# A decode kernel with grouped attention and a dense branch: TensorE's program rolled into a loop over half-groups

## The chip, the cores and the metric

The kernel runs on one NeuronCore of a Trainium2 chip. A core has five engines, each with its own instruction stream: TensorE (PE in the profile; its weight loads are listed apart as PEld), VectorE (DVE), ScalarE (ACT), GpSimd (POOL) and SyncE (SP), which here issues most transfers. Sixteen DMA engines move data between HBM and the on-chip memory SBUF; TensorE writes to a second memory, PSUM. The metric is the device time of one execution in microseconds (us). A profiled execution gives one time beside its span, which runs from its first to its last instruction.

## The reference

One token is decoded. Its normalized row feeds two branches, and both are added to the row.

```python
xn = _layernorm(x)                                  # x: 1 x 512
q = (xn @ wq).reshape(1, 32, 128)                   # 32 heads of 128, wq 512 x 4096
# 8 groups of 4 heads share a key and a value cache of 65536 x 128 each (bf16)
p = softmax(einsum(q, k_cache[g]) * 128 ** -0.5)    # over 65536 keys, per head
A = concat_heads(p @ v_cache[g]) @ wo               # wo 4096 x 512
B = gelu(xn @ w1 + b1) @ w2 + b2                    # w1 512 x 1792, w2 1792 x 512
out = x + A + B
```

The two caches are 2 x 8 x 65536 x 128 values of 2 bytes, 268.4 MB, read once. The weights add 12 MB (wq 4.19, wo 4.19, w1 and w2 3.67).

## The kernel before

**How the order is made.** Python code records every instruction with the tiles that it reads and writes (`sch.op`, `sch.dma`); a recorder (`_Sched`) works out which semaphore waits are needed, and at the end each engine's list is written out in full, one instruction after another. So the order on each engine is that of the Python calls, and TensorE's program holds each of its matmuls once.

**Work and tiles.** For each of the 8 groups the 65536 keys come in 32 transfers of 2 MB (64 tiles of 128 keys x 128 values; line 339 issues them on SP), 16 for K and 16 for V. They land in `cbuf`, a ring of `NB = 8` slots: transfer n goes to slot n mod 8, once TensorE has finished with transfer n - 8. A slot holds two items of 32 tiles.

- A K item is transposed tile by tile on TensorE (line 430, into one of four PSUM tiles `pst`, eight tiles in each). DVE (line 441) or ACT (line 443) copies each filled `pst` to `ktbuf` (the profile's `R_kt`), in the ratio 5 to 3.
- Scores (line 456) multiply each transposed tile with the group's four query columns, two items behind the transposes. They collect in `pss`; DVE copies them to `scf` (line 469) and takes the maximum (line 473).
- When a group's scores are complete, TensorE and DVE turn the maxima into one negated maximum per head for all partitions (`gen_stats_1`, `gen_stats_2`: lines 494, 500, 506, 516, 522), and ACT computes the exps of four heads (line 533, 512 columns each) into `P_bf`, with their sums beside them.
- V items are multiplied with `P_bf` (line 547) and add up in `pB`. V runs one group behind K, so that items of K of group g and of V of group g - 1 alternate, two by two.
- After a group's last V item, TensorE sums the sums over the partitions (line 581), DVE normalizes (lines 585, 589), and 16 matmuls with the group's 512 KB of wo (line 601) add to `finT` (line 611).

The last phase has V items alone. The dense branch runs there: ACT issues the transfers of w1 and w2 (lines 367 and 370) into the transposed keys' memory once that is free; the pieces of the two products (lines 621 to 679) stand between the V items, and gelu between them on DVE and ACT. At the very end the group's epilogue, a transpose (line 782), a copy and the output's transfer (line 790) follow.

At the start SP issues three small rows (x, b1, b2; lines 306 to 310) ahead of the first K chunk, then wq in two transfers (line 351) and further K chunks. The layer norm runs on one partition, and the q projection (line 562) is done after the second K item.

The loop that writes all this down, cut to what sets the order:

```python
for n, it in enumerate(items):        # K,K,(V,V),K,K,(V,V),...
    if kind == "K":
        gen_transposes(i, b, u)
        gen_scores(i - LA); after_scores(i - LA)      # LA = 2
        if had_pending and softmax_q: softmax_q.pop(0)()
    else:
        if softmax_q and softmax_group[0] == g: flush_softmax()
        gen_pv(g, c, b, u)
        if ph == last_phase and pos_in_phase >= 1: ffn_pieces.pop(0)()
    dma_items_upto(dma_cap((n + 1) // NSUB + NB))     # ring of NB = 8
```

Of the kernel before, what the change touches and what calls it, by code (L numbers as in the profile page):

```python
# [5 lines left out]
BF = mybir.dt.bfloat16  # L6
# [4 lines left out]

_DEBUG = {}
# [137 lines left out]

def bass_parallel_sum__gqa_block_cached__dense_activation_gelu__decode_kernel(
# [22 lines left out]
    CH = 4096  # L174
    TPC = CH // 128
    NCH = S // CH
    NKCH = G * NCH
    TPG = NCH * TPC
    BPG = NCH // 4
    assert D % 128 == 0 and F % 128 == 0 and S % CH == 0 and NCH % 4 == 0  # L180
    assert A_k_cache.shape[3] == DH and H % G == 0 and KT == 4 and HPG == 4

    NSUB = 2
    TPD = NSUB * TPC
    NB = 8
    NKT = 4
    NPT = 4
    NPS = 2
    LA = 2
    VLAG = 1  # L190
    NPB = VLAG + 1
# [7 lines left out]
    _DEBUG["sched"] = sch  # L199
# [16 lines left out]
    xrow_bf = nc.alloc_sbuf_tensor("xrow_bf", [1, D], BF)  # L216
    xrow_f = nc.alloc_sbuf_tensor("xrow_f", [1, D], F32)
    junk_row = nc.alloc_sbuf_tensor("junk_row", [1, D], F32)
    st = nc.alloc_sbuf_tensor("st", [1, 8], F32)
    st2 = nc.alloc_sbuf_tensor("st2", [1, 8], F32)  # L220
    xn_row_bf = nc.alloc_sbuf_tensor("xn_row_bf", [1, D], BF)
    xnT_bf = nc.alloc_sbuf_tensor("xnT_bf", [128, KT], BF)
    b1row_bf = nc.alloc_sbuf_tensor("b1row_bf", [1, F], BF)
    b2row_bf = nc.alloc_sbuf_tensor("b2row_bf", [1, D], BF)
    qT_bf = nc.alloc_sbuf_tensor("qT_bf", [128, H], BF)
    h_f = nc.alloc_sbuf_tensor("h_f", [128, FC], F32)
# [6 lines left out]
    call = nc.alloc_sbuf_tensor("cbuf", [128, NB * TPD * DH], BF)  # L233
    cbuf = [call[:, i * TPD * DH:(i + 1) * TPD * DH].rearrange("p (t d) -> p t d", d=DH)
            for i in range(NB)]
    assert KT % NSUB == 0 and TPC * DH == H * DH
    NWQ = KT // NSUB
    WQ_SLOT0 = NB - NWQ
    wq_kt = [call[:, (WQ_SLOT0 * NSUB + kt) * TPC * DH:(WQ_SLOT0 * NSUB + kt + 1) * TPC * DH]
             for kt in range(KT)]  # L240
    wq_slot = [WQ_SLOT0 + kt // NSUB for kt in range(KT)]
    assert CH * NKT >= KT * F + FC * D
    R_kt = nc.alloc_sbuf_tensor("R_kt", [128, NKT * CH], BF)
    ktbuf = [R_kt[:, i * CH:(i + 1) * CH] for i in range(NKT)]
    w1_sb = R_kt[:, 0:KT * F].rearrange("p (kt f) -> p kt f", kt=KT)
    w2_sb = R_kt[:, KT * F:KT * F + FC * D].rearrange("p (fc n) -> p fc n", fc=FC)
    KT_RES_ALL = [f"ktbuf{kb}_{q}" for kb in range(NKT) for q in range(4)]
    wo_g = [nc.alloc_sbuf_tensor(f"wo_g{i}", [128, HPG, D], BF) for i in range(2)]
    scf = [nc.alloc_sbuf_tensor(f"scf{i}", [128, TPG * HPG], F32) for i in range(2)]
    scf_v = [scf[i][:, :].rearrange("p (t j) -> p t j", j=HPG) for i in range(2)]  # L250
    P_bf = [nc.alloc_sbuf_tensor(f"P_bf{i}", [128, TPG * HPG], BF) for i in range(NPB)]
    P_v = [P_bf[i][:, :].rearrange("p (t j) -> p t j", j=HPG) for i in range(NPB)]

    pmax = [nc.alloc_sbuf_tensor(f"pmax{i}", [128, HPG], F32) for i in range(2)]
    pmax_parts = [nc.alloc_sbuf_tensor(f"pmax_parts{i}", [128, BPG * HPG], F32) for i in range(2)]
    gmax4 = [nc.alloc_sbuf_tensor(f"gmax4_{i}", [HPG, 1], F32) for i in range(2)]
    diag4 = [nc.alloc_sbuf_tensor(f"diag4_{i}", [HPG, HPG], F32) for i in range(2)]
    negm = [nc.alloc_sbuf_tensor(f"negm{i}", [128, HPG], F32) for i in range(2)]
    sums = nc.alloc_sbuf_tensor("sums", [128, H], F32)
    rtot = nc.alloc_sbuf_tensor("rtot", [128, H], F32)  # L260
    oT_bf = nc.alloc_sbuf_tensor("oT_bf", [128, H], BF)

# [3 lines left out]
    pB = nc.alloc_psum_tensor("pB", [128, 512], F32)  # L266
    PA_Q = 0
    PA_H = 32
    PA_XN = 48
    PA_SB = 56  # L270
    PA_SUM = 64
# [4 lines left out]
    PB_O = 0  # L276

    csem = [sch.dsem(f"csem{i}") for i in range(NB)]
    sem_misc = sch.dsem("dmisc")
    sem_wq = sch.dsem("dwq")  # L280
    sem_w12 = sch.dsem("dw12")
    sem_out = sch.dsem("dout")


    sch.op(POOL, lambda: pool.memset(ident_bf[:, :], 0.0), writes=["ident_bf"])
    sch.op(
        POOL,
        lambda: pool.affine_select(
            out=ident_bf[:, :], in_=ident_bf[:, :], compare_op=ALU.not_equal, fill=1.0,
            base=0, pattern=[[-1, 128]], channel_multiplier=1,  # L290
        ),
        reads=["ident_bf"], writes=["ident_bf"],
    )
    sch.op(POOL, lambda: pool.memset(ident_f[:, :], 0.0), writes=["ident_f"])
    sch.op(
        POOL,
        lambda: pool.affine_select(
            out=ident_f[:, :], in_=ident_f[:, :], compare_op=ALU.not_equal, fill=1.0,
            base=0, pattern=[[-1, 128]], channel_multiplier=1,
        ),  # L300
        reads=["ident_f"], writes=["ident_f"],
    )
    sch.op(POOL, lambda: pool.memset(ones_f[:, :], 1.0), writes=["ones_f"])
    sch.op(POOL, lambda: pool.memset(finT[:, :], 0.0), writes=["finT"])

    sch.dma(SP, lambda: sp.dma_start(out=xrow_bf[:, :], in_=A_x[0]), sem_misc,
            writes=["xrow_bf"], total=48)
    sch.dma(SP, lambda: sp.dma_start(out=b1row_bf[:, :], in_=B_b1.rearrange("(o n) -> o n", o=1)),
            sem_misc, writes=["b1row"], total=48)
    sch.dma(SP, lambda: sp.dma_start(out=b2row_bf[:, :], in_=B_b2.rearrange("(o n) -> o n", o=1)),  # L310
            sem_misc, writes=["b2row"], total=48)

    NPH = G + VLAG
    items = []
    phase_start = []
    for ph in range(NPH):
        phase_start.append(len(items))
        for c in range(0, NCH + NSUB, NSUB):
            if ph < G and c < NCH:
                items.extend(("K", ph, c + s) for s in range(NSUB))  # L320
            if ph >= VLAG and c >= NSUB:
                items.extend(("V", ph - VLAG, c - NSUB + s) for s in range(NSUB))
    NITEMS = len(items)
    assert NITEMS == 2 * NKCH

    def item_src(it):
        kind, g, c = it
        cache = A_k_cache if kind == "K" else A_v_cache
        return cache[0, g, c * CH:(c + NSUB) * CH, :].rearrange("(p t) d -> p t d", p=128)

    next_item = [0]
    dma_hooks = {}

    def dma_items_upto(n_excl):
        while next_item[0] < min(n_excl, NITEMS // NSUB):
            n = next_item[0]
            b = n % NB
            src = item_src(items[n * NSUB])
            sch.dma(SP, lambda b=b, src=src: sp.dma_start(out=cbuf[b][:, :, :], in_=src),
                    csem[b], writes=[f"cbuf{b}"])  # L340
            for h in dma_hooks.get(n, ()):
                h()
# [511 lines left out]
```

## Time and profile before

| | |
|---|---|
| runs | 690.56 us median of 3 (689.59 to 691.35) |
| profiled execution | 689.94 us; span 688.1 us |
| TensorE's granted clock, mean | 0.792 |
| PE busy | 542.2 us, 12,732 matmuls and as many weight loads |
| DVE, ACT busy | 280.9 us, 243.9 us |
| read from HBM | 280.50 MB |

Rows that begin with a time range are windows: the range, its length, then for PE, PEld, DVE, ACT and POOL the busy us and the number of instructions, then the granted clock, the busy share of the DMA engines and GB/s. Rows "A <- B: x, n, m" are waits: A waited for B x us in all, n times, at most m; "issue" is waiting for nothing that the profile shows. Rows that begin with one time and one duration are the timeline. Rows with "|" are groups of instructions: busy us and mean ns of one, then the idle time ahead. In the rows on the queues, q1 is SP's, q10 ACT's, and q8 and q14 bring instructions: packets, MB, and the share of the sixteen engines' span that the packets took.

### The profile page before, as it was taken

The numbers are of one execution on the slowest core, as the hardware profiler recorded it, in microseconds if no ns is written. First come the engines' busy times: TensorE is split into PE (matmuls) and PEld (weight loads), VectorE is DVE, ScalarE is ACT, GpSimd is POOL, SyncE is SP. The second block draws the span as 40 slices with busy tenths as digits, with TensorE's granted clock in tenths as the row PEclk, the third lists the DMA queues.
The fourth block names the chain that finished last, engine by engine and source line by source line (L and its number), as shares of the span: only waits on it lengthen the run. The fifth ranks groups of instructions, "written<-read, shape, count | busy, mean of one in ns | idle before, by whom it ended". The sixth has DMA issues, their size and how long they took to land.

```text
span 688.1 us, 26439 instructions
## 1 busy us (share of the span) xinstructions
PE 542.2 (79%) x12732; PEld 531.3 (77%) x12732; DVE 280.9 (41%) x457; ACT 243.9 (35%) x266; POOL 1.3 (0%) x10
## 2 busy tenths in 40 slices
PE   3799588886978868887898868888688876887276
PEld 3788588886978868887798868888688876887265
DVE  2276444424444434435444244443344453444001
ACT  4255623325332353325333253332533234332200
POOL 0000000000000000000000000000000000000000
PEclk9799967757898889889879668897797777897555
DMA  8999999999999999999999999999999999999972
GB/s 345 426 426 422 424 423 418 422 427 424 423 416 424 425 422 418 423 424 424 424 417 426 422 424 420 418 426 424 427 418 422 421 425 425 421 424 421 425 310 110
DMA packets 23352, 282.19 MB, mean 410 GB/s; under 512 B 2251, under 2 KB 6349, under 8 KB 6350
## 3 DMA queue, kind: packets, MB, share of 16 engines
q1 hardware_dynamic: 22958, 276.84, 95.7%
q10 hardware_dynamic: 288, 3.67, 1.3%
q8 instruction: 99, 1.62, 1.0%
q14 instruction: 7, 0.06, 0.0%
HBM read 280.50 MB, written 0.00 MB: 408 GB/s over the span
## 4 chain that ended last, share of the span: by engine, by line
PE 64%; DMA 21%; issue 7%; ACT 6%; DVE 1%; SPq 0%
PE pst L430 37%; DMA cbuf<-in_A_k_cache_dram 18%; PE pss L456 12%; PE pB L547 12%; ACT P_bf L533 5%; DMA R_kt<-in_B_w_dram 3%; PE pA L621 1%; PE pA L601 0%; PE pA L494 0%; PE pA L516 0%; PE pA L630 0%; ACT R_kt L443 0%; DVE R_kt L441 0%; PE pA L581 0%; PE pA L661 0%
## 5 line engine op out<-in xcount | busy, mean ns | idle before, releaser
L430 PE MATMUL pst<-ident_bf,cbuf 128*128 128x128 bf16 x4096 | 319.7, 249 | 39.0 <-issue 28.2
L443 ACT ACTIVATE R_kt<-pst 128x1024 bf16<-128x1024 bf16 x192 | 196.6, 1024 | 387.4 <-PE pst L430 387.4
L430 PEld LDWEIGHTS pst<-ident_bf,cbuf 128*128 128x128 bf16 x4096 | 294.2, 114 | 44.6 <-issue 40.1
L441 DVE COPY R_kt<-pst 128x1024 bf16<-128x1024 bf16 x320 | 212.5, 687 | 246.6 <-PE pst L430 246.3
L547 PE MATMUL pB<-P_bf,cbuf 128*128 128x4 bf16 x4096 | 117.5, 165 | 60.3 <-ACT P_bf L533 38.7
L547 PEld LDWEIGHTS pB<-P_bf,cbuf 128*128 128x128 bf16 x4096 | 111.5, 99 | 62.4 <-ACT P_bf L533 39.3
L456 PE MATMUL pss<-qT_bf,R_kt 128*128 128x4 bf16 x4096 | 125.4, 165 | 12.6 <-issue 12.4
L456 PEld LDWEIGHTS pss<-qT_bf,R_kt 128*128 128x128 bf16 x4096 | 121.5, 98 | 13.7 <-issue 13.5
L533 ACT ACTIVATE P_bf<-scf,negm 128x512 bf16<-128x512 f32 x32 | 40.8, 1424 | 6.9 <-DVE negm L522 6.9
L473 DVE TENSOR_REDUCE pmax_parts<-scf 128x4 f32<-128x512 f32 x32 | 34.3, 1071 | 1.1
L469 DVE COPY scf<-pss 128x512 f32<-128x512 f32 x32 | 22.1, 691 | 16.7 <-PE pss L456 16.7
L585 DVE RECIPROCAL rtot<-pA 128x4 f32<-128x4 f32 x8 | 1.5, 182 | 43.4 <-PE pA L581 43.4
L611 DVE TENSOR_TENSOR finT<-pA,finT 128x4 f32<-128x4 f32 x8 | 1.3, 162 | 43.5 <-PE pA L601 43.5
L621 PE MATMUL pA<-xnT_bf,R_kt 128*128 128x1 bf16 x56 | 5.4, 201 | 15.9 <-DMA R_kt<-in_B_w_dram 15.9
L621 PEld LDWEIGHTS pA<-xnT_bf,R_kt 128*128 128x128 bf16 x56 | 4.4, 153 | 16.0 <-issue 15.9
L639 DVE COPY h_f<-pA 128x14 f32<-128x14 f32 x1 | 0.2, 172 | 28.4 <-PE pA L630 28.4
L648 ACT ACTIVATE g_t<-g_t 128x14 f32<-128x14 f32 x1 | 0.2, 215 | 31.2 <-DVE g_t L646 31.2
L533 ACT ACTIVATION_READ_ACCUMULATOR P_bf<-scf,negm 128x1 f32 x32 | 8.1, 253 | 0.0
L562 PE MATMUL pA<-xnT_bf,cbuf 128*128 128x1 bf16 x128 | 3.5, 165 | 4.3 <-DMA cbuf<-in_A_wq_dram 4.3
L562 PEld LDWEIGHTS pA<-xnT_bf,cbuf 128*128 128x128 bf16 x128 | 3.4, 102 | 4.5 <-DMA cbuf<-in_A_wq_dram 4.5
L410 PE MATMUL pA<-ident_bf,xn_row_bf 1*128 1x1 bf16 x4 | 0.3, 172 | 7.4 <-ACT xn_row_bf L403 7.4
L410 PEld LDWEIGHTS pA<-ident_bf,xn_row_bf 1*128 1x128 bf16 x4 | 0.2, 113 | 7.4 <-ACT xn_row_bf L403 7.4
(58 smaller groups left out, 57.6 us busy)
## 6 DMA issues: line engine op xcount, KB each, us to landing
cbuf<-in_A_k_cache_dram SPq DMA_DIRECT2D x64, 2048.0 KB, 29.6
cbuf<-in_A_v_cache_dram SPq DMA_DIRECT2D x64, 2048.0 KB, 30.4
cbuf<-in_A_wq_dram SPq DMA_DIRECT2D x2, 2048.0 KB, 14.5
wo_g<-in_A_wo_dram SPq DMA_DIRECT2D x8, 512.0 KB, 27.8
R_kt<-in_B_w_dram ACTq DMA_DIRECT2D x2, 1792.0 KB, 18.6
xrow_bf<-in_A_x_dram SPq DMA_DIRECT2D x1, 1.0 KB
b1row_bf<-in_B_b_dram SPq DMA_DIRECT2D x1, 3.5 KB
b2row_bf<-in_B_b_dram SPq DMA_DIRECT2D x1, 1.0 KB
```

Source lines behind the costliest of these rows:

```text
L430: lambda tb=tb, slot=slot, b=b, t=t, u=u: pe.transpose(pst[tb][:, slot * 128:(slot + 1) * 128], cbuf[b][:, u + t, :], ident_bf[:, :]),
L441: fn = (lambda tb=tb, dst=dst: dve.tensor_copy(out=dst, in_=pst[tb][:, :]))
L443: fn = (lambda tb=tb, dst=dst: act.activation(out=dst, in_=pst[tb][:, :], func=ACTF.Copy))
L456: lambda sb=sb, slot=slot, kb=kb, t=t, g=g: pe.matmul(pss[sb][:, slot * HPG:(slot + 1) * HPG], lhsT=ktbuf[kb][:, t * 128:(t + 1) * 128], r ...
L469: sch.op(DVE, lambda sb=sb, dst=dst: dve.tensor_copy(out=dst, in_=pss[sb][:, :]), reads=[f"pss{sb}"], writes=[f"scf{gp}_{k4}"])
L473: lambda gp=gp, k4=k4, dst=dst: dve.tensor_reduce(out=pmax_parts[gp][:, k4 * HPG:(k4 + 1) * HPG], in_=dst.rearrange("p (t j) -> p j t", j= ...
L533: lambda gp=gp, gq=gq, g=g, j=j: act.activation(out=P_v[gq][:, :, j], in_=scf_v[gp][:, :, j], func=ACTF.Exp, bias=negm[gp][:, j:j + 1], sc ...
L547: lambda g=g, c=c, b=b, t=t, gp=gp, u=u: pe.matmul(pB[:, PB_O + g * HPG:PB_O + (g + 1) * HPG], lhsT=cbuf[b][:, u + t, :], rhs=P_v[gp][:, c ...
L562: lambda h=h, kt=kt: pe.matmul(pA[:, PA_Q + h:PA_Q + h + 1], lhsT=wq_kt[kt][:, h * DH:(h + 1) * DH], rhs=xnT_bf[:, kt:kt + 1], start=(kt = ...
L585: sch.op(DVE, lambda hs=hs: dve.reciprocal(out=rtot[:, hs], in_=pA[:, PA_SUM:PA_SUM + HPG]), reads=["pA"], writes=[f"rtot{g}"])
L611: lambda: dve.tensor_tensor(out=finT[:, :], in0=pA[:, PA_AT:PA_AT + KT], in1=finT[:, :], op=ALU.add),
L621: lambda fc=fc, kt=kt: pe.matmul(pA[:, PA_H + fc:PA_H + fc + 1], lhsT=w1_sb[:, kt, fc:F:FC], rhs=xnT_bf[:, kt:kt + 1], start=(kt == 0), st ...
```

## The change

The kernel is rewritten around units. A unit is half a group: 32768 keys, four K chunks and four V chunks of 2 MB, so there are 16 units.

- TensorE's program for units 1 to 15 (K of unit u, V of unit u - 1) is recorded 15 times as before, then folded into one body, and written out once inside a loop of 15 rounds (`_fold`, `_emit_loop`). Semaphore values that grow from round to round stand in registers, which are added to between the waits. Unit 0 and the end stand outside. The other engines' programs are written out in full as before.
- Addresses in the body must not change, so slots are fixed: K chunk c of a unit in slot c, V chunk c in slot 4 + c. The transposed keys keep a ring of four, the queries of a unit are copied to one tile `q_cur`, and V adds up in one tile `pO`, which is copied out per unit (`keep_o`).
- Each unit has its own maximum, exps (256 columns) and sums. The two halves of each group are merged at the end: factors exp(min - negm) per half, the sum of the weighted sums, and weighted outputs, on DVE with one exp on ACT.
- wq, w1 and w2 lie at first in the V slots; SP issues them behind the first and the second K chunk, and the dense branch runs within unit 0. wo is kept whole in SBUF, loaded in four pieces of 1 MB by the end of unit 10. All 128 output products of the earlier units stand in the last stage, ahead of the last V chunk.
- The layer norm works on columns: x and b1 come in as columns, x and b2 also as rows, through four small transfers on ACT's queue.

The diff, cut to the parts that set the order:

```diff
+def _emit_loop(eng_obj, ops, growth, n):
...
+    with eng_obj.Fori(0, n):
+        for waits, fn, pub in ops:
+            for s, v in waits:
+                r, now = at[s]
+                if v != now:
+                    eng_obj.reg_add(r, r, v - now)
+                    at[s][1] = v
+                eng_obj.wait_ge(s, r)
+            ins = fn()
+            if pub is not None:
+                ins.then_inc(pub[0], pub[1])
+        for r, step in steps:
+            eng_obj.reg_add(r, r, step)
...
+    def unit(u, first):
...
+        k_block(0)
+        if not first:
+            stats_1()
+        k_block(1)
+        done_chunk("K", 0)
+        if not first:
+            stats_2(u - 1)
+        else:
+            qproj()
+            issue_chunks()
+        load_q(u)
+        k_block(2)
+        scores(u, 0)
+        k_block(3)
+        scores(u, 1)
+        done_chunk("K", 1)
+        v_block(0)
+        v_block(1)
+        if first:
+            ffn1()
+        else:
+            done_chunk("V", 0)
...
+    marks = []
+    unit(0, True)
+    for u in range(1, NU):
+        marks.append(len(PE.ops))
+        unit(u, False)
+    marks.append(len(PE.ops))
...
+    pv(2, 0)
+    wo_part(oT_bf, "oT", list(range(H)))
+    pv(2, 1)
+    pv(3, 0)
+    pv(3, 1)
...
         @block.tensor
         def _(e):
-            replay(PE, e)
+            folded, growth = _fold([PE.ops[a:b] for a, b in zip(marks, marks[1:])])
+            _emit(e, PE.ops[:marks[0]])
+            _emit_loop(e, folded, growth, len(marks) - 1)
+            _emit(e, PE.ops[marks[-1]:])
```

In the rows below a line number is that of the kernel in question, "x32" counts equal instructions in a row, and a wait names its semaphore: `csem` and `dwq` count transfers, `prog_dve`, `prog_act` and `prog_pe` count an engine's instructions.

TensorE before, where a group's softmax falls due (L494 and L516 are its statistics, L547 the V products, which wait for ACT's exps):

```order
L456 MATMUL pss<-qT_bf,R_kt 128x4 x32
L494 MATMUL pA<-ident_f,pmax 4x128 [waits prog_dve]
L430 MATMUL pst<-ident_bf,cbuf 128x128 [waits prog_dve]
L430 MATMUL pst<-ident_bf,cbuf 128x128 x7
L430 MATMUL pst<-ident_bf,cbuf 128x128 [waits prog_act]
```

```order
L456 MATMUL pss<-qT_bf,R_kt 128x4 x32
L516 MATMUL pA<-diag_1,ones_f 128x4 [waits prog_dve]
L547 MATMUL pB<-P_bf,cbuf 128x4 [waits csem2,prog_act]
L547 MATMUL pB<-P_bf,cbuf 128x4 x31
L601 MATMUL pA<-oT_bf,wo_g 128x1 [waits dwo0]
```

TensorE after, the loop's first rows (L210 enters the loop, L215 adds to a register, L538 and L548 are the statistics of the unit before):

```order
L210 UNCONDITIONAL_BRANCH
L484 MATMUL pst<-ident_bf,kv 128x128 [waits csem0]
L484 MATMUL pst<-ident_bf,kv 128x128 x31
L538 MATMUL pA<-ident_f,pmax 4x128 [waits prog_dve]
L215 REGISTER_ALU
L484 MATMUL pst<-ident_bf,kv 128x128 [waits prog_dve]
```

```order
L548 MATMUL pA<-diag,ones_f 128x4 [waits prog_dve]
L215 REGISTER_ALU
L484 MATMUL pst<-ident_bf,kv 128x128 [waits csem1,prog_act]
L484 MATMUL pst<-ident_bf,kv 128x128 x7
L215 REGISTER_ALU
```

The statistics now stand once, in the loop; between the second of them and the first V products lie two blocks of transposes and two of scores (before, nothing); registers are added to between the groups of eight transposes.

TensorE at the end of the program, before:

```order
L547 MATMUL pB<-P_bf,cbuf 128x4 x32
L547 MATMUL pB<-P_bf,cbuf 128x4 [waits csem6]
L547 MATMUL pB<-P_bf,cbuf 128x4 x63
L547 MATMUL pB<-P_bf,cbuf 128x4 [waits csem7]
L547 MATMUL pB<-P_bf,cbuf 128x4 x63
L581 MATMUL pA<-sums,ones_f 128x4 [waits prog_dve]
L601 MATMUL pA<-oT_bf,wo_g 128x1 [waits dwo1,prog_dve]
```

and after (L573 are the V products, L770 those with wo, L788 the final transpose):

```order
L573 MATMUL pO<-P_bf,kv 128x4 [waits csem6]
L573 MATMUL pO<-P_bf,kv 128x4 x31
L770 MATMUL pA<-oT_bf,wo_sb 128x1 [waits dwo,prog_dve]
L770 MATMUL pA<-oT_bf,wo_sb 128x1 x127
L573 MATMUL pO<-P_bf,kv 128x4 x32
L573 MATMUL pO<-P_bf,kv 128x4 [waits csem7]
L573 MATMUL pO<-P_bf,kv 128x4 x63
L770 MATMUL pA<-oL_bf,wo_sb 128x1 [waits prog_dve]
L770 MATMUL pA<-oL_bf,wo_sb 128x1 x15
L788 MATMUL pA<-ident_f,finT 4x128 [waits prog_dve]
```

The sums' product has moved ahead of these rows, 128 products with wo now stand between the two halves of the third V chunk, and 16 remain at the end.

SP at the start of the program, before:

```order
L306 DMA xrow_bf<-in_A_x_dram 1x512
L308 DMA b1row_bf<-in_B_b_dram 1x1792
L310 DMA b2row_bf<-in_B_b_dram 1x512
L339 DMA cbuf<-in_A_k_cache_dram 128x8192
L351 DMA cbuf<-in_A_wq_dram 128x8192 x2
L339 DMA cbuf<-in_A_k_cache_dram 128x8192 x5
```

and after:

```order
L407 DMA kv<-in_A_k_cache_dram 128x8192
L414 DMA kv<-in_A_wq_dram 128x16384
L407 DMA kv<-in_A_k_cache_dram 128x8192
L418 DMA kv<-in_B_w_dram 128x7168
L420 DMA kv<-in_B_w_dram 128x7168
L407 DMA kv<-in_A_k_cache_dram 128x8192 x2
L407 DMA kv<-in_A_k_cache_dram 128x8192 [waits prog_pe] x2
L407 DMA kv<-in_A_v_cache_dram 128x8192
```

The first K chunk is now the first transfer on SP, and the dense weights come behind the second one.

More of the change, by code (lines that the diff above doesn't have):

```diff
@@ L323, in bass_parallel_sum__gqa_block_cached__dense_activation_gelu__decode_kernel @@
[L323 to L342, printed above, removed]
-            next_item[0] += 1
@@ new lines, in stats_2 @@
+    def stats_2(u):
+        k, us = u % 2, slice(u * HPG, (u + 1) * HPG)
+        sch.op(PE, lambda: pe.matmul(pA[:, PA_SB:PA_SB + HPG], lhsT=ones_f[0:HPG, 0:128],
+                                     rhs=diag4[0:HPG, 0:HPG], start=True, stop=True),
+               reads=["diag", "ones_f"], writes=["pA"])
+        sch.op(DVE, lambda us=us: dve.tensor_scalar(out=negm[:, us], in0=pA[:, PA_SB:PA_SB + HPG],
+                                                    scalar1=-1.0, scalar2=None, op0=ALU.mult),
+               reads=["pA"], writes=[f"negm{u}"])
+        for j in range(HPG):
@@ L545, in gen_pv, with pv @@
+                reads=[f"negm{u}"] + [f"scf{k}_{b}" for b in range(NPS)],
+                writes=[f"P_{j}", f"sums{u}_{j}"],
+            )
+    def pv(c, s):
+        b = slot_of["V"] + c
+        for t in range(TPB):
+            tt = s * TPB + t
+            gt = c * TPD + tt
             sch.op(
                 PE,
[L547 to L552 removed]
@@ L618, in gen_ffn1_piece, with ffn1 @@
+        slot_free[NC] = slot_free[NC + 1] = True
+    def ffn1():
+        for fc in range(FC):
             for kt in range(KT):
```

868 lines of the change are left out of this document (402 added, 466 removed).

## The prediction

> **What bounds the kernel now.** I read the page's first sections, then the busy times by window at both ends of the run, then PE's waits.
>
> ```profile
> span 688.1 us, 26439 instructions
> PE 542.2 (79%) x12732; PEld 531.3 (77%) x12732; DVE 280.9 (41%) x457; ACT 243.9 (35%) x266; POOL 1.3 (0%) x10
> DMA  8999999999999999999999999999999999999972
> GB/s 345 426 426 422 424 423 418 422 427 424 423 416 424 425 422 418 423 424 424 424 417 426 422 424 420 418 426 424 427 418 422 421 425 425 421 424 421 425 310 110
> q1 hardware_dynamic: 22958, 276.84, 95.7%
> q8 instruction: 99, 1.62, 1.0%
> HBM read 280.50 MB, written 0.00 MB: 408 GB/s over the span
> ```
>
> The DMA engines are full from the second slice to the 38th and move about 423 GB/s; 280.5 MB at that rate are 663 us. So the transfers bound the kernel, and the other 25 us lie at the ends: about 3 at the start (345 GB/s in slice 1) and the rest in the last two slices (310 and 110 GB/s). The windows of the end show what is missing there:
>
> ```profile
> 659.00:661.00 2.00, 2.00 (x47) 1.93 (x45) 0.00 (x0) 0.00 (x0) 0.00 (x0) 0.50 0.98 403
> 661.00:663.00 2.00, 2.00 (x46) 1.93 (x46) 0.00 (x0) 0.00 (x0) 0.00 (x0) 0.50 0.71 285
> 667.00:669.00 2.00, 2.00 (x49) 1.94 (x49) 0.00 (x0) 0.00 (x0) 0.00 (x0) 0.50 0.46 197
> 677.00:679.00 2.00, 1.52 (x54) 1.46 (x54) 0.16 (x1) 0.00 (x0) 0.00 (x0) 0.50 0.48 189
> 681.00:683.00 2.00, 2.00 (x79) 2.00 (x79) 0.00 (x0) 0.00 (x0) 0.00 (x0) 0.50 0.06 19
> 592.52 46.32 SPq L339 DMA_DIRECT2D cbuf<-in_A_v_cache_dram  x10
> ```
>
> The last value chunk was issued by 638.8 (row of 592.52), so nothing more is asked for. Yet the share falls to a half at 662 and stays there to 680: eight of the sixteen engines are done at about 662, and eight carry on for 18 us more. Every large transfer has 128 partitions and so gives each engine the same bytes; the eight late ones did something else as well. What else there is, is q8: 99 packets of 16.4 KB, that is 1.62 MB for PE's 2 x 12,732 weight loads and multiplies, 64 bytes each, 256 to a packet. They took 1.0% of 16 x 688.1 us, 110 us, 1.11 us each. On eight engines that is 12.4 packets and 13.8 us each, near the 18 that these are late; I put the other 4 down to the change between queues, 1.46 us per packet in all. That only eight engines serve q8 is my inference.
>
> PE shows the same packets. Two windows cut from one pause to the next, and PE's waits:
>
> ```profile
> 343.50:349.93 6.43, 5.47 (x128) 5.20 (x127) 1.38 (x2) 2.05 (x2) 0.00 (x0) 0.56 1.02 418
> 362.50:368.70 6.20, 4.36 (x128) 4.22 (x127) 1.29 (x2) 2.05 (x2) 0.00 (x0) 0.96 1.02 431
> PE pB L547 <- ACT P_bf L533: 38.7, 7, 6.4
> PE pst L430 <- issue: 28.2, 23, 2.4
> PE pB L547 <- issue: 21.6, 16, 2.8
> PE pss L456 <- issue: 12.4, 11, 2.1
> PE pst L430 <- DMA cbuf<-in_A_k_cache_dram: 9.5, 5, 3.5
> ```
>
> The pauses "issue" (62 us, 50 of them) come each 128 matmuls, one packet, never closer than 6.2 us. So PE waits for code: the next packet is asked for when the one before is entered, and arrives about 6.2 us later. PE loses this time without harm, since the ring of eight 2 MB slots covers it: a load lands 29.6 us after its issue, at 5 us of transfer each.
>
> ```profile
> cbuf<-in_A_k_cache_dram SPq DMA_DIRECT2D x64, 2048.0 KB, 29.6
> ```
>
> **The change, part by part.** Base: the profiled execution, 689.94 us, of which 688.1 are the span and 1.84 lie around it; the median of the runs is 0.6 higher.
>
> *Code that is no longer fetched.* PE's program shrinks from 99 packets to 1,526 instructions ahead of the loop, 1,582 in it (770 matmuls, 33 register additions, waits and the branch) and 819 after it: 3,927, or 15.3 packets, if a round of the loop finds its code still there. No row shows PE branching back, so I bound it: all 15 rounds fetched again (no gain here, and the first rival), or none. I take none: 99 packets for 25,464 instructions are one fetch per packet of code, nothing is fetched before it is near, so a fetch looks like the answer to code that is absent. Then the late engines carry 1.9 packets instead of 12.4, 2.8 us, and the last data land at 662 + 2.8 = 664.8 instead of 680. The worth of it has its own bounds: 83 packets x 1.11 us over sixteen engines = 5.8 us if the lag had another cause, 18 if the lag goes entirely. I take 15.2.
>
> *Start.* SP issues the first key chunk first; the three row loads ahead of it go, their successors ride ACT's queue.
>
> ```profile
> 0.74 0.34 SPq L306 DMA_DIRECT2D xrow_bf<-in_A_x_dram  x1
> 1.68 0.36 SPq L339 DMA_DIRECT2D cbuf<-in_A_k_cache_dram  x1
> ```
>
> That is 0.94 us earlier, less 0.3 (estimate; 256 fragments of 8 and 28 bytes for x and b1, bounds 0 to 0.9): gain 0.6. The layer norm on columns and the q projection wait for wq as before. Weights w1, w2 move from ACT's queue near the end to SP's near the start: the same 3.67 MB, no time while the queue is full. In unit 0 SP waits in order for K slots; ahead of it stand 16.2 MB, 38 us, and the first K chunk is used up by about 15 us, so the queue does not run dry.
>
> *Slots.* Each unit issues K0 K1 V0 K2 V1 K3 V2 V3 and uses them up in that order, so eight fixed slots act as the ring of eight did. Cost 0.
>
> *Softmax by halves.* Twice as many maxima, negations and exps, each exp over 256 columns instead of 512:
>
> ```profile
> L533 ACT ACTIVATE P_bf<-scf,negm 128x512 bf16<-128x512 f32 x32 | 40.8, 1424 | 6.9 <-DVE negm L522 6.9
> L500 DVE TENSOR_REDUCE gmax<-pA 4x1 f32<-4x128 f32 x6 | 1.6, 269 | 0.0
> 316.98 1.95 PE L430 MATMUL pst<-ident_bf,cbuf 128*128 128x128 bf16 x32
> 316.18 0.94 PE L456 MATMUL pss<-qT_bf,R_kt 128*128 128x4 bf16 x32
> ```
>
> An exp takes between 0.7 (half) and 1.4 us; I take 1.0 with its read of the sum. Four of them stand on ACT ahead of the eviction that frees PE's second pst bank: PE waits 0.6 + 4 x 1.0 + 1.0 less the 3.1 us that it has to do, 2.5 us per unit, where it waited 38.7 / 7 = 5.5 us per group for P. Some 72 register additions and register waits per round are new on PE. The nearest row is that of the plain semaphore waits, 51 ns at the median, so 3.7 us; bounds 0 (hidden by PE's queue) and the third rival's.
>
> ```profile
> L798 PEldq EVENT_SEMAPHORE  x69: 51/51/2447, 1.5 to 683.4; - x69
> ```
>
> PE's unit at the full clock: 8 x (1.95 + 0.94 + 0.94) = 31 us, plus 2.5, plus 3.7: 37 of the 39.7 us that the 16.8 MB of a unit take at 423 GB/s. So all of this costs nothing on the path; its cover is the ring, and the 62 us of pauses that go. Were the cover gone, each of 15 rounds would add what PE needs beyond 39.7.
>
> *End.* The dense branch is gone from it; the merge of the halves runs on DVE under the last transfers, and 128 of the 144 output products run ahead of the last chunk's. Behind the last landing stand 64 value products and what follows them now, less the sums and the reciprocal (683.77 to 684.59):
>
> ```profile
> 670.64 1.02 PE L547 MATMUL pB<-P_bf,cbuf 128*128 128x4 bf16 x32
> 680.91 2.99 PE L547 MATMUL pB<-P_bf,cbuf 128*128 128x4 bf16 x107 [2.39 <-issue]
> 683.77 0.57 PE L581 MATMUL pA<-sums,ones_f 128*128 128x4 f32 x2
> 684.59 0.16 DVE L589 TENSOR_TENSOR oT_bf<-pB,rtot 128x4 bf16<-128x4 f32 x1
> 686.58 0.29 SPq L790 DMA_DIRECT2D out_dram<-fin_bf  x1
> ```
>
> That is 2 x 1.02 + (688.1 - 684.59) = 5.5 us. The code behind the loop has 3.2 packets, so a pause for code can fall among these products; today's one there was 2.39 us, at 680.91. Bounds 0 and 4; I take 2.0.
>
> *Sum.* The last landing at 664.8 - 0.6 = 664.2; plus 5.5 and 2.0: a span of 671.7. With the 1.84 around it 673.5, and on the scale of the runs' median 674. That is 16.5 us, 2.4%, below 690.56.
>
> **The rivals.** *The loop is fetched again in every round, and PE becomes the bound (slower).* A round touches seven packets of code. At 6.2 us each, one after another, that is 43.4 us, over the 39.7 that the data of a round need. The price: the loop can begin when the first chunk of unit 1 has landed, 2.7 us plus 18.35 MB at 423 GB/s, 46 us; 15 x 43.4 = 651; then 3.2 packets of the end, 20 us: a span of 717, a time of 719. If each round also fetches one packet past its end in vain, 8 x 6.2 x 15 makes it 812. It decides from 6.4 packets a round (39.7 / 6.2); the body has 6.2, the touched ones are seven. For it: the pauses come one packet apart and end with the packet just asked for, so PE works with one packet ahead and may hold little behind. Against it: no row shows a packet fetched twice, though none is needed twice either.
> [...]
>
> *The lag of eight engines is not the code's, or the code is fetched again but in time (hardly faster).* Then the last landing stays at 680, and only start and end change: 680 - 0.6 + 5.5 = a span of 685, a time of 687. For it: nothing in the rows names the eight engines. Against it: 13.8 us of packets beside a lag of 18, and equal bytes otherwise.
>
> *PE's register operations cost more than plain waits (slower).* It decides from (39.7 - 33.5) / 72 = 0.086 us each that PE's queue does not hide; at 0.15 us the round is 44.3 us, and 15 of them make the kernel 15 x (44.3 - 39.7) = 69 us longer, 743. For it: nothing of the kind is in the trace. Against it: the row of 51 ns.
>
> **How the numbers follow.** Forecast 0.66; fetched again 0.22; lag not removed 0.09; register waits 0.03. The forecast's own range is 667 (the lag gone entirely and no pause at the end give 662 - 0.6 + 5.5 + 1.84 = 668.7, and the 662 is read from a window of 2 us) to 682 (half of the lag left). The range for all reaches up to 718, through the 687 and to the edge of the first rival; it leaves out the larger half of that one (0.13), the last (0.03) and some 0.03 below. A measurement of this kernel tells about 0.3%, 2 us, from no change. Faster: 0.66 and half of 0.09, 0.71; within 0.3%: 0.04; slower: 0.25.
>
> **What would show it.** Right: q8 falls from 99 packets to about 16, no pauses "issue" inside the loop, the DMA share full to about 664 and gone within 4 us, the last slice no longer at 7 and 2. The first rival: q8 at 100 or more, a pause at every return of the loop, windows of a round of 43 us or more, the DMA share below 1.00 in the middle. The second: q8 few and the half share at the end still 18 us, or q8 near 100 without gaps. The third: time on PE between groups without any fetch. Half-softmax shown wrong: waits of PE on ACT well above 2.5 us a unit together with gaps in the DMA share. What would make me wrong is above all the return of the loop, which the program before never does.

## The result and the profile after

The changed kernel takes 672.86 us (median of 4 runs, 672.71 to 672.88), the kernel before in the same comparison 690.08 us (689.28 to 691.35): a ratio of 0.9748, 95% interval 0.9731 to 0.9765. The forecast was 674 us. First the page of the changed kernel: the DMA share in 40 slices, what the slices moved, and the queues.

```profile
span 670.9 us, 27090 instructions
PE 556.9 (83%) x12746; PEld 540.2 (81%) x12746; DVE 288.2 (43%) x512; ACT 243.9 (36%) x325; POOL 1.3 (0%) x10
DMA  8999999999999999999999999999999999999994
GB/s 375 414 424 422 427 422 425 429 427 429 420 420 429 425 429 413 426 431 427 426 415 425 430 425 428 415 426 430 427 426 430 428 427 426 428 427 428 427 429 206
q8 instruction: 15, 0.25, 0.1%
```

q8 went from 99 packets to 15, and the two weak slices at the end (310 and 110 GB/s before) became one half slice. The windows of the end, two us each (columns as before: the last two are the DMA share and GB/s), show that the half share that lasted from 662 to 680 is gone within 4 us:

```profile
659.00:661.00 2.00, 0.66 (x24) 0.67 (x25) 0.00 (x0) 0.00 (x0) 0.00 (x0) 0.50 0.95 393
661.00:663.00 2.00, 2.00 (x81) 2.00 (x78) 0.00 (x0) 0.00 (x0) 0.00 (x0) 0.50 0.60 246
663.00:665.00 2.00, 2.00 (x81) 2.00 (x78) 0.16 (x1) 0.00 (x0) 0.00 (x0) 0.50 0.14 57
665.00:667.00 2.00, 2.00 (x81) 2.00 (x78) 0.00 (x0) 0.00 (x0) 0.00 (x0) 0.50 0.03 8
```

PE's waits over the run (without those of the layer norm at the start and of the end): it now waits for data, 54.6 us for keys and 4.9 us for values. The waits "issue", 62 us before, are 5.6 us in all.

```profile
PE pst L484 <- DMA kv<-in_A_k_cache_dram: 54.6, 22, 4.8
PE pst L484 <- ACT kt_ring L494: 23.2, 15, 1.6
PE pO L573 <- DMA kv<-in_A_v_cache_dram: 4.9, 4, 2.1
PE pst L484 <- issue: 2.1, 2, 1.5
PE pO L573 <- issue: 2.1, 1, 2.1
PE pss L505 <- issue: 1.4, 1, 1.4
```

### The profile page after: what moved, and what is told of

It is laid out like the page before. It is cut to its first block, busy times and chain, and to the rows that moved or that the text cites. A ratio compares the mean times of both kernels' runs of the same rounds, so it can differ in the third digit from the quotient of the medians.

```text
span 670.9 us, 27090 instructions
## 1 busy us (share of the span) xinstructions
PE 556.9 (83%) x12746; PEld 540.2 (81%) x12746; DVE 288.2 (43%) x512; ACT 243.9 (36%) x325; POOL 1.3 (0%) x10
## 4 chain that ended last, share of the span: by engine, by line
DMA 54%; PE 39%; ACT 6%; issue 1%; ACTq 0%; DVE 0%; SPq 0%
DMA kv<-in_A_k_cache_dram 49%; PE pst L484 26%; PE pO L573 5%; PE pss L505 5%; ACT P_bf L557 4%; DMA rows_bf<-in_B_b_dram 2%; ACT kt_ring L494 2%; DMA kv<-in_A_v_cache_dram 2%; PE pA L538 1%; PE pA L770 1%; PE pA L606 1%; PE pA L591 0%; PE pA L633 0%; ACTq L445 0%; PE pA L788 0%
## 5 line engine op out<-in xcount | busy, mean ns | idle before, releaser
L484 PE MATMUL pst<-ident_bf,kv 128*128 128x128 bf16 x4096 | 332.9, 255 | 80.1 <-DMA kv<-in_A_k_cache_dram 54.6
L484 PEld LDWEIGHTS pst<-ident_bf,kv 128*128 128x128 bf16 x4096 | 306.7, 117 | 90.6 <-issue 32.4
L494 ACT ACTIVATE kt_ring<-pst 128x1024 bf16<-128x1024 bf16 x192 | 194.7, 1022 | 381.7 <-PE pst L484 381.7
L492 DVE COPY kt_ring<-pst 128x1024 bf16<-128x1024 bf16 x320 | 213.1, 688 | 266.0 <-PE pst L484 265.6
L573 PE MATMUL pO<-P_bf,kv 128*128 128x4 bf16 x4096 | 117.1, 165 | 10.4 <-DMA kv<-in_A_v_cache_dram 4.9
L505 PE MATMUL pss<-q_cur,kt_ring 128*128 128x4 bf16 x4096 | 122.9, 165 | 1.4 <-issue 1.4
L573 PEld LDWEIGHTS pO<-P_bf,kv 128*128 128x128 bf16 x4096 | 111.8, 99 | 10.9 <-DMA kv<-in_A_v_cache_dram 5.2
L505 PEld LDWEIGHTS pss<-q_cur,kt_ring 128*128 128x128 bf16 x4096 | 118.7, 98 | 1.5 <-issue 1.5
L557 ACT ACTIVATE P_bf<-scf,negm 128x256 bf16<-128x256 f32 x64 | 49.6, 862 | 7.2 <-DVE negm L551 7.2
L538 PE MATMUL pA<-ident_f,pmax 128*4 128x128 f32 x32 | 8.5, 364 | 0.4 <-DVE pmax L525 0.4
L548 PEld LDWEIGHTS pA<-diag,ones_f 4*128 4x128 f32 x32 | 4.9, 190 | 2.7 <-DVE diag L542 1.1
L548 PE MATMUL pA<-diag,ones_f 4*128 4x4 f32 x32 | 6.3, 264 | 0.6 <-DVE diag L542 0.6
L538 PEld LDWEIGHTS pA<-ident_f,pmax 128*4 128x4 f32 x32 | 1.4, 84 | 3.2 <-DVE kt_ring L492 2.5
```

Source lines behind the costliest of these rows:

```text
L484: lambda tb=tb, at=at, b=b, tt=s * TPB + t: pe.transpose(pst[tb][:, at * 128:(at + 1) * 128], slot[b][:, tt, :], ident_bf[:, :]),
L492: e, fn = DVE, lambda tb=tb, dst=dst: dve.tensor_copy(out=dst, in_=pst[tb][:, :])
L494: e, fn = ACT, lambda tb=tb, dst=dst: act.activation(out=dst, in_=pst[tb][:, :], func=ACTF.Copy)
L505: lambda sb=sb, col=col, kb=kb, t=t: pe.matmul(pss[sb][:, col * HPG:(col + 1) * HPG], lhsT=kt_ring[:, kb * BCOL + t * 128:kb * BCOL + (t + ...
L538: sch.op(PE, lambda: pe.matmul(pA[0:HPG, PA_ST:PA_ST + 128], lhsT=pmax[:, 0:HPG], rhs=ident_f[:, :], start=True, stop=True), reads=["pmax" ...
L548: sch.op(PE, lambda: pe.matmul(pA[:, PA_SB:PA_SB + HPG], lhsT=ones_f[0:HPG, 0:128], rhs=diag4[0:HPG, 0:HPG], start=True, stop=True), reads ...
```

## The experiments

Three theories were open after the result, and a fourth came up on the way. A: the gain is the code, which rides on some of the engines that carry the data, and the loop's code stays held. B: the gain comes from the rest of the rewrite (order, slots, dense branch in front, shorter end). C: it is not the number of packets that costs, but that code is fetched at all while the data run. D, after the fourth run: what is held goes by the length of the loop's body, not by the packets that it touches. Each experiment is the changed kernel with one edit.

**The loop written out in full.**

```diff
-            folded, growth = _fold([PE.ops[a:b] for a, b in zip(marks, marks[1:])])
-            _emit(e, PE.ops[:marks[0]])
-            _emit_loop(e, folded, growth, len(marks) - 1)
-            _emit(e, PE.ops[marks[-1]:])
+            _emit(e, PE.ops)
```

> The changed kernel with TensorE's loop written out in full: the same operations in the same order, some 25,500 instructions of PE, 100 packets of code instead of 15. Theory A (the half share at the end is the price of code that rides eight of the sixteen DMA engines, 1.46/8 = 0.18 us of lateness a packet): 85 packets more make eight engines late by 15.5 us, the half share is back from about 661 to 677, pauses 'issue' one packet apart are back on PE, time about 688 us. Rival B (the gain came from the order, the dense branch in front, the softmax by halves and the shorter end): 673 us, no half share, although q8 shows 100 packets.

Measured: 690.7 us (690.33 to 691.0, 10 runs), 0.9998 of the kernel before (0.9982 to 1.0013). The whole gain is gone, though everything else of the rewrite is in place. The page of this run:

```profile
GB/s 366 425 425 424 423 425 423 426 425 423 409 423 425 424 423 406 423 425 425 423 385 421 426 424 422 403 428 425 423 425 423 424 421 425 425 423 423 404 328 131
q8 instruction: 99, 1.62, 1.0%
```

Its last six issues of value chunks in the timeline of SP's queue:

```profile
622.01 42.87 SPq L407 DMA_DIRECT2D kv<-in_A_v_cache_dram  x6
```

And windows of its end:

```profile
659.00:661.00 2.00, 0.37 (x15) 0.28 (x12) 0.00 (x0) 0.00 (x0) 0.00 (x0) 0.78 0.53 213
667.00:669.00 2.00, 0.00 (x0) 0.00 (x0) 0.41 (x3) 2.00 (x5) 0.00 (x0) 0.50 1.00 426
677.00:679.00 2.00, 1.98 (x74) 1.99 (x75) 0.00 (x0) 0.00 (x0) 0.00 (x0) 0.50 0.52 221
679.00:681.00 2.00, 1.96 (x74) 1.88 (x71) 0.00 (x0) 0.00 (x0) 0.00 (x0) 0.50 0.11 41
```

The share is at a half twice: around 660, when the last chunk is not yet issued (the row at 622.01 ends at 664.88, as SP waited for PE's value products to free the slot), and again before 679. In the windows from 657 on it never falls clearly below a half until 679: half of the engines have work all the time and set the end. The packets kept in the trace say the same: the last packet of data ended at 681.4 us, against 664.7 in the changed kernel. PE's pauses are back too:

```profile
PE pO L573 <- issue: 37.4, 20, 2.8
PE pss L505 <- issue: 24.6, 15, 3.1
PE pst L484 <- issue: 9.7, 9, 2.1
```

B falls: the rest of the rewrite is worth nothing that this measurement can tell. A's figure was 2.7 us low, 0.21 us a packet (17.8 us for 84) instead of 0.18; this kernel's end has a pause for code of 0.76 us among its last products as well.

**Half of the units written out.**

```diff
+            del marks[:7]      # units 1 to 7 written out, 8 to 15 in the loop
```

> The changed kernel with units 1 to 7 of TensorE written out and 8 to 15 in the loop: some 14,700 instructions, 57 packets of code. Theory A: 42 packets more than the changed kernel, 0.18 us each, 7.7 us: about 680.5 us, eight engines late by half as much as with all units written out. Rival B: 673 us. A third theory C (what costs is not the number of packets but that any code is fetched while the data run, for instance at the very end): the time of the fully written-out or of the fully looped kernel, not one halfway.

Measured: 680.66 us (680.45 to 680.82), ratio 0.9859 (0.9841 to 0.9877). Its queue of code, then windows of its end:

```profile
q8 instruction: 57, 0.93, 0.6%
```

```profile
663.00:665.00 2.00, 1.71 (x64) 1.72 (x64) 1.49 (x8) 0.00 (x0) 0.00 (x0) 0.50 0.73 303
665.00:667.00 2.00, 0.16 (x6) 0.07 (x3) 0.00 (x0) 0.00 (x0) 0.00 (x0) 0.50 0.50 205
669.00:671.00 2.00, 2.00 (x82) 2.00 (x78) 0.00 (x0) 0.00 (x0) 0.00 (x0) 0.50 0.50 205
671.00:673.00 2.00, 2.00 (x82) 2.00 (x78) 0.16 (x1) 0.00 (x0) 0.00 (x0) 0.50 0.04 16
```

42 packets more cost 7.8 us, 0.186 us each; the half share lasts some 7 us, from 664 to 671. Cost and lag go with the number of packets, so C falls. By the packets kept in the trace, 54 of the 57 were fetched by 386 us of the 679, and the lag is seen at the end (the last packet of data ended at 672.6 us): what the late engines had lost by 386 us was not given back in the 285 us to the end of the half share.

**Two units in the loop's body.**

```diff
+            del marks[1::2]    # 7 rounds of two units, unit 15 written out
```

> The changed kernel with two units in the body of TensorE's loop (7 rounds of units 1 to 14, unit 15 written out): a body of some 3,160 instructions, 12.4 packets, 13 or 14 touched; 7,050 instructions in all. If code stays held whatever the size of the loop: q8 at 27 to 29 packets, 675 us. [...]

Measured: 743.02 us (741.84 to 747.68), ratio 1.0785 (1.0745 to 1.0825), 7.9% slower than the kernel before, which has no loop. The page, and PE's waits over the run:

```profile
GB/s 370 425 427 421 424 425 422 422 424 418 418 422 418 363 409 423 424 347 358 410 426 423 294 379 409 426 422 301 391 414 362 366 306 368 418 397 388 201 273 130
q8 instruction: 111, 1.82, 1.0%
```

```profile
PE pst L484 <- issue: 53.0, 19, 6.4
PE pss L505 <- issue: 38.3, 20, 3.5
PE pO L573 <- issue: 34.7, 17, 3.6
```

111 packets are the 27 of the program and 84 more: six returns times 14, the 13 touched and one past the end. The pauses reach 126 us, the GB/s fall in the middle. This is the first rival of the prediction, met by a loop of twice the size: holding has a limit, between 7 and 13 touched packets.

**At the edge: 100 products more in each unit.**

```diff
+                   pe.matmul(pA[:, 448:452], lhsT=ident_bf[:, :], rhs=ident_bf[:, 0:4], ...)
...
         scores(u, 5)
+        if not first:
+            junk(100)
```

> The changed kernel with 100 further products of the identity in each unit of the loop, into a part of PSUM that nothing reads: a body of some 1,780 instructions, 7.0 packets, 8 touched. [...] If eight packets and the one fetched ahead fit: q8 at 16, 673 us, since PE's unit of some 35 to 37 us stays under the 39.5 of the data. If the edge is passed: q8 at 130 or more, 8 x 6.2 = 50 us a round, 15 rounds, 800 us or more. If PE had no room left in its unit (my sum for PE put 2.7 us of slack): between 673 and 680 us with q8 at 16 and a DMA share below 1.00 in the middle.

Measured: 731.61 us (726.55 to 743.58), ratio 1.0598 (1.0565 to 1.0631). Its queue of code; then two successive rounds as windows, from return to return; then PE's longest wait "issue" in the first of the two (in the second there is none). `junk(n)` stands, here and below, for n such products.

```profile
q8 instruction: 79, 1.29, 0.8%
```

```profile
142.00:191.40 49.40, 36.45 (x886) 35.32 (x887) 18.14 (x31) 15.03 (x20) 0.00 (x0) 0.74 1.01 419
191.40:231.50 40.10, 34.52 (x861) 33.52 (x859) 17.27 (x30) 15.03 (x20) 0.00 (x0) 0.76 1.01 425
```

```profile
PE pst L484 <- issue: 9.9, 3, 6.6
```

None of the three expectations: 79 packets are neither 16 nor 130. They are the 16 of the program and 63 more, 7 times 9: every second round fetches its eight packets and one past the end, and the rounds between fetch nothing. With seven touched packets and one past the end there was no such fetching (15 packets in all). What becomes of a packet between two rounds no trace shows; theory A of the next run is an inference from these counts. The packets kept in the trace fit them by their times: one starts at 140.5 us, just ahead of the return at 142, eight more from 141.4 to 186.8, then none until 230.0. Why the packet past the end comes only in every second round, no trace shows.

**The same loop, moved.** Body of the changed kernel, moved by 194 instructions ahead of it.

```diff
     unit(0, True)
+    junk(97)
```

> The changed kernel, its loop of 1,582 instructions untouched, with 97 products of the identity (194 instructions, 2.6 us of PE, once, into a part of PSUM that nothing reads) between unit 0 and the loop. They only move the loop's code by 0.76 packets: it starts at 0.97 of a packet instead of 0.21, so it touches eight packets instead of seven. Theory A (eight packets are held, the oldest is given up first, and one is fetched past the loop's end): 8 + 1 do not fit, whole rounds are fetched again, every second one as with the 100 products in the loop; q8 at 75 or more, rounds of about 50 and 37 us in turn, time 715 to 730 us. If all rounds are fetched again, 780 or more. Rival D (what counts is the length of the body, and 6.2 packets fit while 7.0 do not, or the longer round of PE made the difference there): q8 at 16, 673 us.

Measured: 736.0 us median (727.79 to 740.98), ratio 1.0615 (1.0539 to 1.0691). The profile is that of the longest run, 740.98 us. Its queue of code, and again two successive rounds:

```profile
q8 instruction: 79, 1.29, 0.8%
```

```profile
145.30:200.00 54.70, 36.29 (x795) 34.79 (x796) 18.52 (x31) 15.43 (x21) 0.00 (x0) 0.69 0.93 374
200.00:237.50 37.50, 33.40 (x752) 32.40 (x750) 17.08 (x29) 14.62 (x20) 0.00 (x0) 0.73 1.00 419
```

The code of the loop is the same, and 2.7 us of work stand outside it, yet the kernel loses 63 us against the unmoved one. D falls: the place of the code decides. Theory A had the count (75 packets or more expected, 79 measured) and the two kinds of round in turn; which packet is given up first, no run shows. Its time was 6 us low by the median. In this profile, of the longest run, the round that fetches takes nearer 54 than 50 us; whether that holds for the others is not shown. That 64 packets more cost 63 us here, and 84 more only 17.8 with the loop written out, has another cause than the late engines: here the packets crowd into every second round. In the first round shown, eight of them start one after another from 146.2 to 194.7 us (from 141.4 to 186.8 with the 100 products), longer than the 39.5 us that the data of a unit take, so PE falls behind and the DMA share falls too (0.93).

**The longer loop, aligned.** A body of 6.9 packets that begins just behind a packet's border.

```diff
     unit(0, True)
+    junk(107)
...
         scores(u, 5)
+        if not first:
+            junk(90)
```

> The changed kernel with 90 products of the identity in each unit of the loop (a body of 1,762 instructions, 6.9 packets) and 107 ahead of the loop, so that the body starts at 0.05 of a packet and ends at 0.93: it touches seven packets. Theory A: 7 + 1 fit in eight, so q8 at 17 and, since the products cost PE 2.4 us a unit where it waits 3.6 us for data, 673 us; at most 676 if PE's room is smaller. Rival D (the length of the body counts): as with the 100 products before, q8 near 79 and 725 us.

Measured: 674.57 us (672.84 to 675.92), ratio 0.9772 (0.9742 to 0.9801). Its queue of code, and PE's wait for keys:

```profile
q8 instruction: 17, 0.28, 0.2%
```

```profile
PE pst L484 <- DMA kv<-in_A_k_cache_dram: 34.1, 20, 5.9
```

180 instructions longer than the loop that failed when it was moved, and not fetched again in its rounds (17 packets): it touches seven. The products cost PE some of its wait for data (54.6 us before them) and the kernel 1.7 us by the medians; the profiled run, 672.84 us, shows nothing of that.

**The dense branch back at the end.**

```diff
-    after_chunk[("K", 0, 1)] = [dma_w12]
+    after_chunk[("V", NU - 1, 0)] = [dma_w12]      # into key slots 0 and 1
...
     pv(0, 1)
+    ffn1()                                         # no longer in unit 0
...
     pv(1, 1)
+    ffn2()
```

> The changed kernel with the dense branch back at the end: w1 and w2 go into key slots 0 and 1 after the first value chunk of the last unit, the products of the branch stand among the last value products; the loop stays. If the place of the dense branch is worth nothing, as the run with the loop written out suggests (all of the gain is the code): 673 us. If the branch in front took PE's work from the end: 116 products of 33 ns are 3.8 us, and a pause for its code 2 us more, so up to 677 to 679 us.

Measured: 675.74 us (674.15 to 675.86), ratio 0.9783 (0.9758 to 0.9808), 2.9 us above the changed kernel. The timeline of PE's end, with the wait ahead in brackets:

```profile
663.06 2.54 PE L766 MATMUL pA<-oT_bf,wo_sb 128*128 128x1 bf16 x90 [0.82 <-issue]
667.07 1.68 PE L573 MATMUL pO<-P_bf,kv 128*128 128x4 bf16 x58 [0.46 <-issue]
```

Two pauses for code, 1.3 us together, now fall among the last products. The profiled run is the fastest of the four, 1.4 us above the changed kernel's, so the pauses explain that run; what the other three lose beyond it no trace shows. So the dense branch in front is worth 1.4 to 3 us once the data end early. With the loop written out the rest of the rewrite as a whole was worth nothing measurable; the dense branch alone was not tried there.

**More work for PE at the same code.** 24 products of 400 columns a unit (`junk` here), seven packets as before.

```diff
+                   pe.matmul(pO[:, 112:512], lhsT=ident_bf[:, :], rhs=zz[:, :], ...)
...
+        if not first:
+            junk(24)
         v_block(0)
```

> The changed kernel with 24 products of 400 columns in each unit of the loop, into a part of PSUM that nothing reads. 48 instructions more, so the code stays at seven packets, but PE gets work: a transpose of 128 columns takes 61 ns at the full clock, so 400 columns some 0.19 us and 24 of them 4.6 us a unit (5.9 us at the granted clock of 0.77). The prediction put PE at 37 of 39.7 us, 2.7 us of room: then each of 15 rounds is 1.9 to 3.2 us longer, 702 to 721 us, with gaps in the DMA share. If PE's room is the 3.6 us a round that it waits for data in the trace of the changed kernel: 1.0 to 2.3 us a round, 688 to 708 us. If PE has 6 us or more of room: 673 us.

Measured: 673.09 us (672.79 to 673.79), ratio 0.9742 (0.9717 to 0.9767): no loss. The groups of the added products and of the transposes, PE's wait for keys, and 400 us of the middle as a window, of this kernel; then the transposes and the same window of the changed one:

```profile
L658 PE MATMUL pO<-zz,ident_bf 128*128 128x400 bf16 x361 | 67.9, 347 | 0.0
L486 PE MATMUL pst<-ident_bf,kv 128*128 128x128 bf16 x4096 | 304.4, 242 | 41.9 <-ACT kt_ring L496 23.2
```

```profile
PE pst L486 <- DMA kv<-in_A_k_cache_dram: 18.1, 9, 3.0
```

```profile
200.00:600.00 400.00, 364.19 (x8090) 335.67 (x8088) 179.18 (x304) 152.39 (x202) 0.00 (x0) 0.85 1.01 426
```

```profile
L484 PE MATMUL pst<-ident_bf,kv 128*128 128x128 bf16 x4096 | 332.9, 255 | 80.1 <-DMA kv<-in_A_k_cache_dram 54.6
200.00:600.00 400.00, 332.50 (x7664) 322.37 (x7662) 175.00 (x298) 149.49 (x200) 0.00 (x0) 0.77 1.01 426
```

The products took 67.9 us, 4.5 a unit. 36.5 us of them came out of PE's wait for keys (54.6 to 18.1). The granted clock rose from 0.77 to 0.85 (0.843 to 0.852 over the span in all four runs, 0.770 to 0.800 in the nine of the changed kernel), and the transposes took 28.5 us less (332.9 us in the changed kernel, 304.4 here): that is the other part. That they took less by the clock is the likely reading, and why the clock rose is open. Of the three cases in the expectation the last came, but not by 6 us of room: PE had waited 4 us a unit for data, and the shorter transposes gave the rest.

**A shorter end**, beside the changed kernel once more (the last two lines of the edit are simplified).

```diff
+    wo_part(oT_bf, "oT", list(range(H)))
     pv(2, 0)
-    wo_part(oT_bf, "oT", list(range(H)))
     pv(2, 1)
...
+    sp.dma_start(out=slot[b][:, 0:48, :], in_=src[:, 0:48, :])      # last V chunk in two transfers
+    sp.dma_start(out=slot[b][:, 48:, :], in_=src[:, 48:, :])
```

> The changed kernel with a shorter end: the 128 output products stand ahead of the last unit's third value chunk (PE is idle there for 2.07 us) instead of behind it, and the last value chunk comes in two transfers of 48 and 16 of its 64 columns, so that 16 products (0.5 us) instead of 64 (2.0 us) follow the last landing. In the changed kernel's trace PE ends its value products at 667.33 with the last data at about 665.2; 16 products after 665.2 end at 665.7: 1.6 us earlier, 671.3 us against 672.9, 0.24%. If the last landing itself moves (two transfers, their fixed costs), or a pause for code falls among the last products: no gain that can be told, 672.5 to 674 us.

> The changed kernel once more, as the measure for the shorter end on the same chip: 672.9 us, ratio 0.975.

Measured: 672.37 us (672.06 to 672.54) and 672.79 us (672.75 to 672.90). The shorter end is faster by 0.42 us, 0.06%, a quarter of what I expected. First the end of the changed kernel, then that of this one:

```profile
660.34 1.02 PE L573 MATMUL pO<-P_bf,kv 128*128 128x4 bf16 x32 [2.07 <-DMA kv<-in_A_v_cache_dram]
661.21 3.55 PE L770 MATMUL pA<-oT_bf,wo_sb 128*128 128x1 bf16 x128
664.63 2.70 PE L573 MATMUL pO<-P_bf,kv 128*128 128x4 bf16 x96
```

```profile
661.56 1.68 PE L777 MATMUL pA<-oT_bf,wo_sb 128*128 128x1 bf16 x57 [1.07 <-issue]
663.10 2.03 PE L579 MATMUL pO<-P_bf,kv 128*128 128x4 bf16 x71
665.30 1.68 PE L579 MATMUL pO<-P_bf,kv 128*128 128x4 bf16 x57 [0.17 <-issue]
```

In the changed kernel nothing waits for the last data: from 660.34 on PE works without a gap, output products first, then 96 value products. I had taken the last landing for the release; by the packets kept in the trace it came at 664.7, when 96 products were still to do. Here the output products start earlier, at 658.44, but a pause for code of 1.07 us falls among them, and PE again works until 667. It is the fastest version measured, by an amount that is not worth its code.

## Why the prediction was right, step by step

*What bounds the kernel* was read rightly: eight engines late at the end by what they had carried besides the data. That the half share is the code's is shown by the kernels with 99 and 57 packets. The "eight", an inference in the prediction, is borne out by the packets kept in the trace of the kernel before. Between 500 and 510 us 16.2 of them are under way at a time on average, between 664 and 671 us 8.3, and never fewer than eight. The times of the packets of code recur with every eighth: one differs from the eighth after it by 1 ns at the median, from the first to seventh after it by 13 to 47 ns. That large transfers load the engines equally fits the changed kernel's trace: its first key chunk is 128 packets of 16 KB in sixteen chains of eight, and the share falls from 0.95 to 0.14 within 4 us at the end. The trace does not name the engines, so that the eight late ones are those that bring the code is inferred from the lag, which goes with the number of packets.

*Code no longer fetched* (99 to 15.3 packets, last landing 664.8, 15.2 us) was the main term, and right: 15 packets, and the last packet of data ended at 664.7 us, where the sum with its gain at the start had 664.2. The price of 1.46 us a packet on an engine, 0.18 at the end, was measured as 0.186 with half of the units written out and as 0.21 with all; by the last packets of data (672.6 and 681.4) it is 0.188 and 0.199. The part of that price that the prediction put down to the change between queues, 0.35 us a packet, is a remainder that no run took apart.

*The loop stays held* was right, but that it fits was luck: the argument for it (a fetch answers absent code) holds for a loop of any size, and the loop with two units in its body was fetched again in every round. By the counts there is no packet to spare: the loops that touch seven, and one past their end, were not fetched again (15 and 17 packets), the two that touch eight were in every second round (79 each). The rival's condition in the prediction was wrong: I put its edge where fetching takes longer than a round's data, 6.4 packets a round, and its price at 719 us. The edge measured lies between seven touched packets and eight, and just behind it the kernel takes 726 to 744 us with every second round fetched.

*Start* (0.6): slice 1 moved 375 instead of 345 GB/s. Against a full rate, 427 and 423, 2.0 us are missing in it instead of 3.2 (16.77 us x (1 - 375/427); 17.20 x (1 - 345/423)), so the gain was about 1.1; the 0.3 that the prediction took off for the small fragments was my estimate, and no run shows it. *Slots* (0): right, the share is still 0.95 in the window from 659 to 661.

*Softmax by halves and register operations* cost nothing on the path, as predicted, but the sizes were off. An exp with its read of the sum takes 0.75 us from one start to the next, not 1.0; four of them take 1 us less than I put, and PE waits 23.2 / 15 = 1.5 us a unit for ACT, not 2.5.

```profile
176.41 0.87 ACT L557 ACTIVATE P_bf<-scf,negm 128x256 bf16<-128x256 f32 x1
177.16 0.86 ACT L557 ACTIVATE P_bf<-scf,negm 128x256 bf16<-128x256 f32 x1
```

The 3.7 us a round for register waits are not to be found: all "issue" waits of the run are 5.6 us, and 32 transposes in the loop take 1.95 us (at 161.52 in the timeline) as in the kernel before. The 495 register additions take 32 ns each at the median on PE's sequencer, hidden behind the matmuls, and the third rival (743) is not met. PE's unit of 37 us still came near the 35.5 measured (39.5 less 4 of waiting for data, where I left 2.7), and that too is in part luck: against these two terms stands a third that I put too low, the transposes at the full clock. At the 0.77 granted they take 332.9 / 16 = 20.8 us a unit, not 8 x 1.95 = 15.6.

*End* (5.5 and a pause of 2.0): from the 64 value products I expected behind the last landing it became PE's own chain from 660.34 to 670.9. No pause for code fell in it, but 32 more value products stand behind the output products. The step was wrong: it is the third value chunk's landing at 660.34 that releases this chain, not the last landing. The run ends 0.8 us ahead of the forecast's span of 671.7 all the same, 6.2 us behind the last landing where I put 7.5. That is luck as far as the end goes; the main term did not need it.

## What to carry to other kernels

When a kernel is bound by transfers, look at the DMA share behind the last issue and at the instruction queue: a share that stays at a fraction can mean that some engines also carried code, here 0.19 to 0.21 us of delay for each 16.4 KB packet of TensorE's program. A loop removed it here only where its code was not fetched again, and that went by the packets that the loop touches from its place in the program, not by its length: with seven and one past the end 15 and 17 packets were fetched in all, with eight and one 79. So read the queue's packet count after each edit ahead of or inside the loop. The loop that missed by one packet was worse than no loop: 6% slower than the kernel without one.

## What the runs showed of the hardware that I had not expected

- Moving a held loop by 194 instructions cost 63 us of 673 (79 packets instead of 15), and the misses came in every second round.
- The delay of the late engines adds up over the run: 54 of 57 packets were fetched by 386 us, and their delay was still 7 us of half share at its end, from 664 to 671.
- With 4.5 us more of long products in each unit the granted clock was 0.85 instead of 0.77, and the time was the same within 0.3 us.
